# Chained waits between GpSimd's compute operations, in a fused linear-attention, Fourier-mix and MLP kernel

## Chip, cores and metric

The kernel runs on one core of a Trainium2 chip. The metric is device time in microseconds (us) for one execution, lower is better. Engines are named as in the profile: PE is TensorE, DVE is VectorE, ACT is ScalarE, POOL is GpSimd, SP is the engine that issues most transfers.

## What is computed

A gated linear attention over 768 steps feeds a Fourier mix, a layer norm and an MLP, for 4 batches:

```python
for t in range(S):                                   # S = 768, 8 heads of 48
    cur = einsum('bhd,bhe->bhde', u * k[t], v[t])
    y[t] = einsum('bhd,bhde->bhe', r[t], state + cur)
    state = w * state + einsum('bhd,bhe->bhde', k[t], v[t])
x = y as [4, 768, 384]
un = layer_norm(x + real(fft(fft(x, axis=1), axis=2)))
out = (x + mixed) + relu(un @ w_ch1) @ w_ch2         # 384 -> 1536 -> 384
```

## The kernel before

The sequence is cut into chunks of 128 steps, 24 in all (6 for each of 4 batches). For one chunk, `attend` multiplies k and r by tables of powers of w (tile KR, line 385), transposes them (on PE, line 409, or by a transposing transfer of SP, line 415; tile KRT), forms the scores (line 443), masks them (AC and MA, lines 450 to 455), and adds the masked product with V (line 534), the carried state S (line 513) and the bonus of u (PR at line 431, de at line 507 with the small table UW, TT at line 522) into one bank. The result is X. The chunks of a batch are folded by even and odd symmetry (EO, HH, XF, lines 557 to 593), go through the two Fourier products (lines 635 and 676, with tiles TT2 and TR), and become UF, its scaled copy UB (line 700 on POOL) and, transposed (line 720 on PE with the copy at line 727, or by SP at line 746), UNT. The MLP then runs by halves of a batch: `mlp1` at line 764, `mlp2` at line 785, the result osb at line 795 and its transfer out at line 798.

No scheduler decides the order. Each operation is recorded with one or more alternatives (an engine, a key, a function), and the long table `ORDER` lists number and alternative in the order of issue; `_Schedule.emit` walks it, assigns buffers of the rings to tiles and calls the function. Each engine then runs its instructions in that order, and waits on semaphores are set where one instruction reads, or writes over, what another made. Instructions of one engine are not made to wait for the one just ahead unless such a dependence is found.

POOL has 91 compute operations (copies, masks, products) and issues 24 transfers: four small ones of w and u into the tile wuc at the start (line 301), five of the MLP's weights (lines 839 and 842), and 15 of results. wuc is used on DVE, where UW is formed (line 338), and on ACT, where the logarithm lwc is taken (line 329). An instruction carries one wait; where it needs more, the others stand in a wait instruction (EVENT_SEMAPHORE) ahead of it.

Of the kernel before, what the change touches and what calls it, by code (L numbers as in the profile page):

```python
# [9 lines left out]
AluOp = mybir.AluOpType  # L10
# [5 lines left out]
H = 8  # L16
S = 768
D = 48
# [33 lines left out]
class _Tile:  # L52


    def __init__(self, ring, view=None):
        self.ring, self.view, self.value = ring, view, None
# [5 lines left out]
class _Schedule:  # L62


    def __init__(self):
        self.ops, self.rings = [], {}

    def ring(self, name, tiles):
        self.rings[name] = tiles
# [1 line left out]
    def op(self, name, alts, r=(), w=(), new=(), use=(), after=(), uses=None, link=None):  # L71
        self.ops.append(dict(name=name, alts=alts, r=list(r), w=list(w), new=list(new), use=list(use), after=list(after),
                             uses=uses or [[] for _ in alts], link=link))

    def emit(self, order):
        last = {}
        for k, (n, a) in enumerate(order):
            o = self.ops[n]
            for t in o["new"] + o["use"] + o["uses"][a]:
                last[t] = k  # L80
        held = {name: [-1] * len(tiles) for name, tiles in self.rings.items()}
        for k, (n, a) in enumerate(order):
            o = self.ops[n]
            for t in o["new"]:
                ends = held[t.ring]
                m = min(range(len(ends)), key=ends.__getitem__)
                assert ends[m] < k, (o["name"], t.ring)
                ends[m] = last[t]
                t.value = self.rings[t.ring][m] if t.view is None else t.view(self.rings[t.ring][m])
            fn = o["alts"][a][2]  # L90
            if fn is not None:
                fn()


ORDER = """
# [74 lines left out]
def kernel(  # L170
# [11 lines left out]
    nc = tc.nc  # L182
# [5 lines left out]
    hid_c = nc.inline_tensor(hid_n, name="hid_c")  # L188

    sch = _Schedule()  # L190
    op = sch.op
    sch.ring("bank", [ps.tile([128, 512], F32, name=f"bank{i}") for i in range(8)])

# [60 lines left out]
    def T(name, view=None):  # L254
        return _Tile(name, view)
# [115 lines left out]
    def attend(i):  # L371
# [3 lines left out]
        KR, V, KRT, PR = T("KR"), T("V"), T("KRT"), T("PR")  # L375
# [3 lines left out]
        def scaled(s):  # L379
            return (KR()[:, s].rearrange("t p (a d) -> t (p a) d", a=2)[:, :, 0:D], kr()[:, s],  # L380
                    wtab[ph][:, s].rearrange("t (h d) -> t h d", d=D))

        def scale(eng, s):
            o, x, y = scaled(s)
            eng.tensor_tensor(out=o, in0=x, in1=y, op=AluOp.mult)  # L385

        def both():
            nc.vector.tensor_tensor(
# [6 lines left out]
        for s, nm in ((0, "k"), (1, "r")):  # L395
            dve = ("DVE", "K1", lambda s=s: scale(nc.vector, s))
            pool = ("POOL", "K1", lambda s=s: scale(nc.gpsimd, s))
            op(("KR", i, s), [VOID, dve, pool if s else dve, dve if s else pool], r=[(nm, i), ("wt", ph, s)] + zeroed,
               w=[("KR", i, s)], use=[kr, KR], after=[("KR", i)], link=("KR", i))
# [11 lines left out]
        for s, dn in ((0, kdone), (1, qdone)):  # L411
# [4 lines left out]
            out=KRT().rearrange("d s p t -> d (s p) t"), in_=KR().rearrange("t s p c -> t (s p c)")))],  # L416
# [86 lines left out]
        DE, TT = T("DE"), T("TT")  # L503
# [15 lines left out]
           uses=[[yd], []])  # L519

        def spread(eng, x):
            eng.tensor_tensor(out=TT(), in0=V(), in1=x.unsqueeze(2).to_broadcast([128, H, D]), op=AluOp.mult)

        op(("TT", i), [("POOL", "TT", lambda: spread(nc.gpsimd, DE())), ("DVE", "TTp", lambda: spread(nc.vector, yd()[:, DM:]))],
           r=[("DE", i), ("V", i), ("de", i)], w=[("TT", i)], new=[TT], use=[V], uses=[[DE], [yd]], link=("DE", i))
        if q > 0:
            one(("qs", i), "PE", "qs", carried, r=[("S", i), ("de", i)] + kts, use=[yd, St, KRT])

        def intra():
# [13 lines left out]
            out=X()[:, q, :], in0=yd()[:, 0:DM], in1=TT().rearrange("p h d -> p (h d)"), op=AluOp.add)),  # L543
# [76 lines left out]
    def fourier(b):  # L620
        X, XF = bat[b]["X"], bat[b]["XF"]
        TT, TR = T("TT2"), T("TR")
# [28 lines left out]

        def rev(g):
            def turn(eng):
                eng.tensor_copy(TR()[0:97, 2 * g:2 * g + 2, :], TT()[0:97, 2 * g:2 * g + 2, 384:0:-1])

            op(("TR", b, g), [("DVE", "TR", lambda: turn(nc.vector)), ("POOL", "TR", lambda: turn(nc.gpsimd)),
                              ("ACT", "TR", lambda: nc.scalar.copy(
                                  TR()[0:97, 2 * g:2 * g + 2, :], TT()[0:97, 2 * g:2 * g + 2, 384:0:-1]))], w=[("TR", b, g)],
                r=[("TT2", b, 2 * g), ("TT2", b, 2 * g + 1)], new=[TR] if g == 0 else [], use=[TR, TT],
                after=[("TR", b, 0)] if g else [])  # L660
# [70 lines left out]
        for sh in range(2):  # L731
# [12 lines left out]
            for j in range(3):  # L744
                turned(sh, j, UB, UNT)
            op(("UNT", b, sh), [VOID, VOID, VOID, VOID, ("SP", "xbar9", lambda UB=UB, UNT=UNT: nc.sync.dma_start_transpose(
                out=UNT().rearrange("p j c t -> p (j c) t"), in_=UB().rearrange("p j d -> p (j d)")))],
# [79 lines left out]
    for i in range(NC):  # L827
# [5 lines left out]
                  out=tn_t, in0=te_t[:, :, :, 1, :], scalar1=-1.0, scalar2=None, op0=AluOp.mult))], r=["te"], w=["tn"])  # L833
# [4 lines left out]
    for n in range(2):  # L838
        one(("W1", n), "POOL", "dma_w1", lambda n=n: nc.gpsimd.dma_start(
            out=W1[:, :, n * 768:(n + 1) * 768], in_=w1[:, n * 768:(n + 1) * 768].rearrange("(c p) f -> p c f", p=128)))  # L840
    for n in range(3):
        one(("W2", n), "POOL", "dma_w2", lambda n=n: nc.gpsimd.dma_start(
            out=W2[:, n * 4:(n + 1) * 4, :], in_=w2[n * 512:(n + 1) * 512, :].rearrange("(p f) d -> p f d", f=4)))
# [37 lines left out]
```

## Time and profile before

| | us |
|---|---|
| median of 3 runs | 174.22 (174.11 to 176.03) |
| the profiled execution | 174.01 |
| its span, first to last instruction | 172.3 |
| PE busy | 155.3 |
| DVE busy | 136.6 |
| ACT busy | 108.2 |
| POOL busy | 82.0 |

The profiled execution is 174.01 us; 1.7 us of it lies outside the span. Times in rows are us from the span's start. A row of a timeline gives start, duration, engine, line, operation, and, in brackets, how long the engine sat idle ahead of it and what ended that. The matmuls' ends are modelled, so that a busy PE is one that has been fed, not one at its peak.

### The profile page before, as it was taken

How to read it: one execution, taken by the hardware profiler on the slowest of the kernel's cores; microseconds unless marked ns; L12 is line 12 of the kernel's file. 1: busy time of each engine (PE TensorE's matmuls, PEld its weight loads, DVE VectorE, ACT ScalarE, POOL GpSimd, SP SyncE). 2: the span in 40 equal slices, each digit the busy share in tenths (PEclk: the TensorE clock that was granted, in tenths of full speed). 3: DMA queues.
4: the chain of work that ended last, by engine and by line, in shares of the span. 5: the costliest groups of instructions: out<-in, count | busy, mean ns of one | idle time of the engine just before them, and what ended most of it. 6: DMA issues, size and time to landing. Idle time of an engine off the chain costs nothing.

```text
span 172.3 us, 4247 instructions
## 1 busy us (share of the span) xinstructions
PE 155.3 (90%) x1586; PEld 111.6 (65%) x1586; DVE 136.6 (79%) x320; ACT 108.2 (63%) x258; POOL 82.0 (48%) x119
## 2 busy tenths in 40 slices
PE   4367977689999999999999999999999999999990
PEld 1155755559767776877666687677776876666670
DVE  4489999987798989999579999968899689630460
ACT  2976786448988697656993577578861850922400
POOL 7277387814828980778376473466330122000131
PEclk9999999978999999999999999999999999999999
DMA  5999999999698999999999959999500236200132
GB/s 115 212 209 212 232 200 242 149 189 201 119 198 173 188 166 173 221 212 212 216 187 237 214 104 194 237 199 181 200 3 0 94 68 181 73 4 0 46 137 91
DMA packets 97782, 27.08 MB, mean 157 GB/s; under 512 B 94369, under 2 KB 96434, under 8 KB 97762
## 3 DMA queue, kind: packets, MB, share of 16 engines
q1 hardware_dynamic: 92336, 21.01, 63.0%
q0 software_dynamic: 2304, 5.21, 13.0%
q10 hardware_dynamic: 3122, 0.59, 2.1%
q8 instruction: 12, 0.20, 0.5%
q14 instruction: 8, 0.07, 0.1%
HBM read 19.77 MB, written 4.72 MB: 142 GB/s over the span
## 4 chain that ended last, share of the span: by engine, by line
PE 54%; issue 23%; DVE 11%; DMA 4%; POOL 4%; SPq 1%; POOLq 0%; ACT 0%; DVEq 0%
PE bank L764 19%; PE bank L785 14%; DMA kr<-in_r_dram 4%; PE bank L635 4%; PE bank L676 3%; PE bank L443 3%; PE bank L409 2%; DVE KR L385 2%; POOL out_dram L798 2%; PE bank L474 2%; PE bank L534 2%; PE bank L513 2%; DVE MA L455 1%; DVE XF L566 1%; DVE PR L431 1%
## 5 line engine op out<-in xcount | busy, mean ns | idle before, releaser
L764 PE MATMUL bank<-UNT,W 128*128 128x384 bf16 x288 | 54.8, 327 | 0.0
L785 PE MATMUL bank<-W,HT 128*128 128x384 bf16 x276 | 52.0, 326 | 0.0
L769 ACT ACTIVATE HT<-bank 128x384 bf16<-128x384 f32 x73 | 33.5, 491 | 21.8 <-PE bank L764 21.6
L764 PEld LDWEIGHTS <-W 128*128 128x128 bf16 x288 | 30.5, 114 | 11.7
L785 PEld LDWEIGHTS <-HT 128*128 128x128 bf16 x276 | 25.8, 98 | 14.1
L385 DVE TENSOR_TENSOR KR<-kr,wtab 128x384 bf16<-128x384 f32 x30 | 21.4, 727 | 3.8 <-ACT wtab L325 2.9
L798 POOL DMA_DIRECT2D out_dram<-osb x14 | 8.0, 572 | 33.9 <-DVE osb L795 33.9
L452 POOL TENSOR_SCALAR_AFFINE_SELECT MA<-AC 128x512 bf16<-128x512 bf16 x25 | 16.3, 657 | 8.7 <-ACT AC L450 8.6
L385 POOL TENSOR_TENSOR KR<-kr,wtab 128x384 bf16<-128x384 f32 x14 | 15.2, 1090 | 10.6 <-DMA kr<-in_r_dram 5.0
L795 DVE SCALAR_TENSOR_TENSOR osb<-bank,rstd,UF 128x384 f32<-128x384 f32 x23 | 13.5, 610 | 7.9 <-PE bank L785 6.8
L450 ACT CAST AC<-bank 128x512 bf16<-128x512 f32 x25 | 14.2, 587 | 6.8 <-PE bank L443 5.8
L770 DVE TENSOR_SCALAR HT<-bank 128x384 bf16<-128x384 f32 x23 | 12.3, 548 | 6.8 <-PE bank L764 6.7
L455 DVE TENSOR_TENSOR MA<-bank,mtri 128x512 bf16<-128x512 f32 x23 | 15.3, 680 | 1.1 <-PE bank L443 1.1
L409 PE MATMUL bank<-ident,KR 128*128 128x128 bf16 x112 | 12.0, 253 | 3.9 <-DVE UW L311 1.8
L419 ACT COPY KRT<-bank 128x512 bf16<-128x512 bf16 x20 | 11.2, 589 | 5.2 <-PE bank L409 5.0
L635 PE MATMUL bank<-te_t,XF 128*128 128x193 bf16 x108 | 12.2, 251 | 2.1 <-DVE XF L566 1.2
L409 PEld LDWEIGHTS <-KR 128*128 128x128 bf16 x112 | 8.8, 114 | 6.4 <-DVE UW L311 3.0
L431 POOL TENSOR_TENSOR PR<-KRT 128x512 bf16<-128x512 bf16 x7 | 8.1, 1156 | 10.2 <-ACT KRT L419 9.7
L707 ACT ACTIVATE tn_t<-UF,sm 128x384 bf16<-128x384 f32 x21 | 12.9, 613 | 0.1
L635 PEld LDWEIGHTS <-XF 128*128 128x128 bf16 x120 | 10.4, 100 | 3.5 <-DVE XF L566 1.6
L688 DVE SCALAR_TENSOR_TENSOR UF<-bank,X 128x384 f32<-128x384 f32 x21 | 11.0, 552 | 1.6 <-PE bank L676 1.6
L542 DVE TENSOR_TENSOR X<-bank,TT 128x384 bf16<-128x384 f32 x18 | 9.6, 550 | 2.6 <-PE bank L534 2.5
(110 smaller groups left out, 259.8 us busy)
## 6 DMA issues: line engine op xcount, KB each, us to landing
kr<-in_k_dram SPq DMA_DIRECT2D x23, 192.0 KB, 4.1
kr<-in_r_dram SPq DMA_DIRECT2D x23, 192.0 KB, 4.1
vt<-in_v_dram SPq DMA_DIRECT2D x23, 192.0 KB, 4.2
out_dram<-osb POOLq DMA_DIRECT2D x14, 192.0 KB, 3.0
out_dram<-osb SPq DMA_DIRECT2D x9, 192.0 KB, 2.5
W<-in_moe_w_ch_dram POOLq DMA_DIRECT2D x2, 576.0 KB, 8.4
W<-in_moe_w_ch_dram POOLq DMA_DIRECT2D x3, 384.0 KB, 5.6
te_t<-te_c SPq DMA_DIRECT2D x1, 579.0 KB, 5.9
```

The source lines that it names most:

```text
L385: eng.tensor_tensor(out=o, in0=x, in1=y, op=AluOp.mult)
L409: nc.tensor.transpose(tps[s]()[:, p, :], KR()[:, s, p, :], ident)
L450: op(("AC", i, a), [("ACT", "AC", lambda: nc.scalar.copy(AC(), A_ps[a]())), ("NONE", "", None)], r=[("A", i)], w=[("AC", i, a)], new=[AC], ...
L452: op(("MA", i, a), [("POOL", "MA", lambda: nc.gpsimd.affine_select(out=MA[a](), in_=AC(), pattern=[[0, NP], [1, 128]], base=0, channel_mul ...
L455: ("DVE", "MA", lambda: nc.vector.tensor_tensor(out=MA[a](), in0=A_ps[a](), in1=mtri.unsqueeze(1).to_broadcast([128, NP, 128]), op=AluOp.m ...
L635: nc.tensor.matmul(fp()[:, par, :], lhsT=lhsT[:, g * CH:g * CH + 128], rhs=rhs, start=(nb == 0 and par == 0), stop=(nb == last and par == ...
L707: ("ACT", "SQ", lambda: nc.scalar.activation(out=squares, in_=UF()[:, j, :], func=Act.Square, scale=-float(DM), bias=sm()[:, j:j + 1], acc ...
L764: nc.tensor.matmul(hp(), lhsT=W1[:, dt, ft // 4 * 512 + ft % 4:(ft // 4 + 1) * 512:4], rhs=UNT()[:, :, dt, :], start=(dt == 0), stop=(dt = ...
L769: op(("HT", hf, ft), [("ACT", "HT", lambda: nc.scalar.activation(out=HT()[:, ft, :], in_=hp(), func=Act.Relu, scale=-1.0)), ("DVE", "HT", ...
L770: ("DVE", "HT", lambda: nc.vector.tensor_scalar(out=HT()[:, ft, :], in0=hp(), scalar1=-1.0, scalar2=0.0, op0=AluOp.mult, op1=AluOp.max))],
L785: nc.tensor.matmul(mo(), lhsT=HT()[:, ft, j * 128:(j + 1) * 128], rhs=W2[:, ft, :], start=(ft == 0), stop=(ft == 11))
L795: one(("osb", hf, j), "DVE", "osb", lambda: nc.vector.scalar_tensor_tensor(out=osb(), in0=mo(), scalar=rstd()[:, j:j + 1], in1=UF()[:, j, ...
```

## The change

Each compute operation of POOL is given a wait for POOL's compute operation ahead of it, and where POOL has issued one or more transfers in between, an empty instruction (`engine_nop`) is put behind them, and the next compute operation waits for that one. The order of everything else stays.

```diff
-            fn = o["alts"][a][2]
+            eng, key, fn = o["alts"][a]
             if fn is not None:
-                fn()
+                if eng != "POOL":
+                    fn()
+                elif key.startswith("dma"):
+                    fn()
+                    self.issued = True
+                else:
+                    self.chain(fn, self.issued)
+                    self.issued = False
...
+    last = []
+
+    def chain(fn, issued):
+        if issued:
+            last.append(nc.gpsimd.engine_nop())
+        made = fn()
+        if last:
+            tc.add_manual_dep(made.ins, last[-1].ins.name,
+                              mybir.DependencyInfo(mybir.DependencyClass.Sync, mybir.DependencyReason.DATA),
+                              reason="all cores of GpSimd done")
+        last.append(made)
+
+    sch.chain = chain
...
-            eng.tensor_tensor(out=o, in0=x, in1=y, op=AluOp.mult)
+            return eng.tensor_tensor(out=o, in0=x, in1=y, op=AluOp.mult)
```

Three helpers (`scale`, `spread`, `turn`) return their instruction, so that it can be chained. In the built program, 89 of the 91 compute operations wait for POOL's own semaphore (Pool_49) where 16 did, 15 empty instructions are new, and POOL's wait instructions go from 48 to 97. The programs of PE, DVE, ACT and SP have the same instructions in the same order, with waits on the same semaphores.

At the start of POOL's program, where the four transfers into wuc stand among the first fills (S_98 and the like are buffers; DVE_49, Activation_49, DMAHW4_49 the semaphores of DVE, ACT and a transfer), before:

```order
L301 DMA wuc<-in_u_dram 48x4x1 [waits DVE_49]
L319 MEMSET S_98 128x384
L301 DMA wuc<-in_w_dram 48x4x1
L288 AFFINE_SELECT ident<-HT_186 128x128 [waits DVE_49]
L319 MEMSET S_95 128x384
L301 DMA wuc<-in_u_dram 48x4x1
```

and now, lines counted in the changed kernel (ISA at L202 is the empty instruction):

```order
L321 DMA wuc<-in_u_dram 48x4x1 [waits DVE_49]
L202 ISA
L339 MEMSET S_98 128x384 [waits Pool_49]
L321 DMA wuc<-in_w_dram 48x4x1
L202 ISA
L308 AFFINE_SELECT ident<-HT_186 128x128 [waits DVE_49,Pool_49]
L339 MEMSET S_95 128x384 [waits Pool_49]
L321 DMA wuc<-in_u_dram 48x4x1
```

Two empty instructions and three waits now stand ahead of the third transfer into wuc.

On POOL again, at the first blocks of UB (batch 0, ahead of the first MLP product), before:

```order
L431 TENSOR_TENSOR PR_123<-KRT_120 128x512 [waits Activation_49]
L700 TENSOR_SCALAR UB_179<-UF_148,sm_163 128x384 [waits Activation_49]
L700 TENSOR_SCALAR UB_179<-UF_148,sm_163 128x384 [waits DVE_49]
L700 TENSOR_SCALAR UB_180<-UF_149,sm_164 128x384 [waits Activation_49]
L522 TENSOR_TENSOR TT_141<-V_117,DE_138 128x384 [waits Activation_49]
```

and now:

```order
L451 TENSOR_TENSOR PR_123<-KRT_120 128x512 [waits Activation_49,Pool_49]
L720 TENSOR_SCALAR UB_179<-UF_148,sm_163 128x384 [waits Activation_49,Pool_49]
L720 TENSOR_SCALAR UB_179<-UF_148,sm_163 128x384 [waits DVE_49,Pool_49]
L720 TENSOR_SCALAR UB_180<-UF_149,sm_164 128x384 [waits Activation_49,Pool_49]
L542 TENSOR_TENSOR TT_141<-V_117,DE_138 128x384 [waits Activation_49,Pool_49]
```

The order is the same; each has a second wait, for its predecessor on POOL, and so a wait instruction ahead of it for the first one.

## Rows read from the trace of the kernel before

**Rows 1.** The page's busy times: engine, busy us, share, instructions.
```profile
PE 155.3 (90%) x1586; PEld 111.6 (65%) x1586; DVE 136.6 (79%) x320; ACT 108.2 (63%) x258; POOL 82.0 (48%) x119
```

**Rows 2.** Busy time by stretch: window, its length, busy us of each engine.
```profile
9.40:36.00 26.60, 19.62 (x276) 15.22 (x273) 25.88 (x59) 17.93 (x41) 18.64 (x28) 1.00 1.08 206
36.00:46.00 10.00, 9.96 (x133) 8.42 (x131) 8.44 (x23) 8.06 (x22) 4.54 (x7) 0.83 0.98 179
46.00:126.00 80.00, 80.00 (x863) 57.28 (x862) 70.92 (x153) 60.41 (x147) 47.82 (x63) 1.00 0.97 191
```

**Rows 3.** Timeline of POOL, the start, with the transfers into wuc.
```profile
1.54 0.77 POOL L301 DMA_DIRECT2D wuc<-in_u_dram  x1 [0.50 <-DVE wuc L295]
2.31 0.44 POOL L319 MEMSET S<- 128x384 bf16 x1
2.67 0.60 POOL L301 DMA_DIRECT2D wuc<-in_w_dram  x1
3.28 0.30 POOL L288 TENSOR_SCALAR_AFFINE_SELECT ident<-HT 128x128 bf16<-128x128 bf16 x1
3.53 0.42 POOL L319 MEMSET S<- 128x384 bf16 x1
3.89 0.61 POOL L301 DMA_DIRECT2D wuc<-in_u_dram  x1
```

**Rows 4.** The tile wuc: its transfers from issue to landing.
```profile
DMA to landing us min/median/max: 4.3/5.2/5.4
```

**Rows 5.** Timeline of DVE where it uses wuc.
```profile
9.42 0.16 DVE L338 TENSOR_TENSOR UW<-wuc 64x4 bf16<-64x4 f32 x1 [0.29 <-DMA wuc<-in_u_dram]
9.75 0.56 DVE L385 TENSOR_TENSOR KR<-kr,wtab 128x384 bf16<-128x384 f32 x1 [0.17 <-DMA kr<-in_r_dram]
```

**Rows 6.** Timeline of POOL, two XF in a row, the second waiting for the first.
```profile
28.35 0.51 POOL L566 TENSOR_TENSOR XF<-HH 128x196 bf16<-128x196 bf16 x1 [0.93 <-DVE HH L560]
...
28.94 0.57 POOL L566 TENSOR_TENSOR XF<-HH 128x196 bf16<-128x196 bf16 x1
```

**Rows 7.** The chain of waits near 24 and 125 us: start, us, what.
```profile
23.55 0.07 issue
23.61 0.51 POOL XF L566
...
124.88 0.02 POOLq L522
124.90 0.10 issue
```

**Rows 8.** Timeline of POOL, very small fills at the program's start.
```profile
0.31 0.10 POOL L865 MEMSET const-float32-0.0<- 128x1 f32 x1 [0.31 <-issue]
0.34 0.10 POOL L865 MEMSET const-float32-1.0<- 128x1 f32 x1
```

**Rows 9.** Timeline of POOL at the first blocks of UB.
```profile
40.85 1.16 POOL L431 TENSOR_TENSOR PR<-KRT 128x512 bf16<-128x512 bf16 x1 [5.74 <-ACT KRT L419]
41.99 0.58 POOL L700 TENSOR_SCALAR UB<-UF,sm 128x384 bf16<-128x384 f32 x1
...
42.70 0.59 POOL L700 TENSOR_SCALAR UB<-UF,sm 128x384 bf16<-128x384 f32 x1
```

**Rows 10.** Timeline of PE, the transposes of those blocks.
```profile
42.72 0.33 PE L720 MATMUL bank<-ident,UB 128*128 128x128 bf16 x3
...
43.34 0.51 PE L720 MATMUL bank<-ident,UB 128*128 128x128 bf16 x6
```

**Rows 11.** Timeline of POOL, then of PE, at a mask in the dense stretch.
```profile
52.74 0.64 POOL L452 TENSOR_SCALAR_AFFINE_SELECT MA<-AC 128x512 bf16<-128x512 bf16 x1
...
53.88 0.36 PE L534 MATMUL bank<-V,MA 128*128 128x48 bf16 x8
```

**Rows 12.** Timeline of DVE near 116 us.
```profile
116.37 0.55 DVE L522 TENSOR_TENSOR TT<-V,bank 128x384 bf16<-128x384 bf16 x1 [0.53 <-POOL V L402]
```

More of the change, by code (lines that the diff above doesn't have):

```diff
@@ L65, in __init__ @@
     def __init__(self):
-        self.ops, self.rings = [], {}
+        self.ops, self.rings, self.issued = [], {}, False
     def ring(self, name, tiles):
@@ L521, in spread @@
         def spread(eng, x):
-            eng.tensor_tensor(out=TT(), in0=V(), in1=x.unsqueeze(2).to_broadcast([128, H, D]), op=AluOp.mult)
+            return eng.tensor_tensor(out=TT(), in0=V(), in1=x.unsqueeze(2).to_broadcast([128, H, D]), op=AluOp.mult)
         op(("TT", i), [("POOL", "TT", lambda: spread(nc.gpsimd, DE())), ("DVE", "TTp", lambda: spread(nc.vector, yd()[:, DM:]))],
@@ L653, in turn @@
             def turn(eng):
-                eng.tensor_copy(TR()[0:97, 2 * g:2 * g + 2, :], TT()[0:97, 2 * g:2 * g + 2, 384:0:-1])
+                return eng.tensor_copy(TR()[0:97, 2 * g:2 * g + 2, :], TT()[0:97, 2 * g:2 * g + 2, 384:0:-1])
             op(("TR", b, g), [("DVE", "TR", lambda: turn(nc.vector)), ("POOL", "TR", lambda: turn(nc.gpsimd)),
```

## The prediction

> **What bounds the kernel now.** I read the busy times first: PE is busy 155.3 of 172.3 us, POOL 82.0 [rows 1]. The share is an average, so I read the busy times by stretch next. From 46 to 126 us PE is busy 80.00 of 80.00 us, and from 36 to 46 us 9.96 of 10.00: there PE's own stream, in a fixed order, sets the end, and whatever delays it once is not won back. From 9.4 to 36 us DVE is busy 25.88 of 26.60 us, PE only 19.62: there DVE's stream sets when the first Fourier products and so the MLP can begin [rows 2]. POOL is never the busiest engine. So a slower POOL costs time only where DVE or PE stands waiting for something that POOL made or sent, and the question is where that is with less cover than POOL is late.
>
> **What one wait costs.** Two operations in a row without a wait: the second starts before the first one's row ends, by 0.05 us (3.28 + 0.30 against 3.53) [rows 3] or 0.02 (40.85 + 1.16 against 41.99) [rows 9]. The trace holds one pair in which the second already waits for the first: 28.35 + 0.51 = 28.86, and it starts at 28.94, 0.08 us later [rows 6]. So a wait between neighbours that are both ready costs 0.08 + 0.05 = 0.13 us (0.10 with the smaller overlap).
>
> Where POOL stood idle for another engine, the wait for its predecessor is long met, but the other engine's semaphore is now awaited in a wait instruction of its own. Directly, an operation starts 0.07 us after its release; through a wait instruction 0.02 + 0.10 = 0.12 us after that instruction began [rows 7]. That costs 0.05 us.
>
> An empty instruction is not in the trace of before. The nearest rows are fills of one element: 0.10 us long, but started 0.03 us apart [rows 8]. I take 0.10, because a wait sees the end and not the start, and 0.08 for the wait behind it: 0.18 us, since the fill behind a transfer starts now just as the transfer's row ends (1.54 + 0.77 = 2.31) [rows 3]. From below it could be nothing, if the empty instruction overlaps; from above I bound it by the transfer's own row, 0.77 + 0.08 = 0.85 us. The row of the small fill is nearer in kind, as neither moves data, so 0.18 stands.
>
> In total POOL gets at most 89 x 0.13 + 15 x 0.10 = 13 us more, 95 of 172 us: it does not become the bound by its sum. What counts are two places.
>
> **Place one, the transfers into wuc.** Ahead of the third transfer stand now two empty instructions and one wait between neighbours (select, then fill); the transfers themselves wait for nothing new. It is issued 2 x 0.18 + 0.13 = 0.49 us later than at 3.89 [rows 3]. Such transfers take 4.3 to 5.4 us to land [rows 4], and DVE waits for one of them: it sat idle 0.29 us ahead of UW at 9.42. So nothing covers the 0.49 us there; but the operation after next, KR at 9.75, sat idle 0.17 us for its own transfer, which now swallows 0.17 [rows 5]. What is left on DVE is 0.49 - 0.17 = 0.32 us. Queued behind UW on DVE is everything that PE needs. In the stretch to 36 us DVE is idle 0.72 us, of which the two gaps named are 0.46; the other 0.26 [rows 2, 5] could swallow most of it if those gaps are waits for transfers or for an engine that has not moved; I take it that PE, fed by DVE, moves along, and keep 0.32, with 0.06 as the low end. ACT, too, takes a logarithm of wuc; its delay runs beside that of DVE and is not added.
>
> **Place two, the first UB.** PR at 40.85 was released by ACT: now through a wait instruction, +0.05. UB at 41.99 follows it directly: +0.13. It ends at 42.75 instead of 42.57, and PE's transposes of it, at 42.72 now [rows 9, 10], begin 0.18 us later. The second UB then starts at 42.75 + 0.08 = 42.83 instead of 42.70, +0.13 [rows 9]; its transposes at 43.34 [rows 10] have by then moved 0.18 with PE's stream, so this is covered. +0.18 us, in a stretch where PE has no idle time to give [rows 2].
>
> **Elsewhere.** After 46 us I found no product of POOL for which PE waits. The closest is a mask that ends at 52.74 + 0.64 = 53.38 and is used at 53.88: 0.50 us of cover [rows 11], against one wait of 0.13. The masks, copies and products around it come in runs of two to four between idle times of POOL, so lateness of 0.3 to 0.5 us builds up and is given back. DVE waits once, 0.53 us at 116.37 [rows 12], where the copy that it needs comes 0.05 us later; DVE has 9 us idle in that stretch [rows 2]. I cost all this at nothing; if its cover fails at one place, that is 0.1 to 0.4 us. The last transfers have no compute operation of POOL behind them, hence no empty instruction.
>
> **Sum.** 0.32 + 0.18 = 0.50 us. On the profiled execution, 174.01 us (span 172.3 and 1.7 around it), that makes 174.5; the median of the runs is 0.2 us above that execution, so I forecast 174.7 us, which a measurement of this kernel can hardly tell from no change (2% is about 3.5 us).
>
> [...] With a free empty instruction the first place gives 0.13, less than the 0.17 of cover, and the sum is 0.18 us.
>
> **Rivals.**
> - *All hidden, or the waits cost nothing.* The empty instruction is free, 0.13 us at wuc stays under the 0.17 of cover, and UB's 0.18 is all: 174.22 + 0 to 0.18, 174.3 us. For it: the gaps of DVE that I left out, 0.26 us. Against it: the pair of XF shows a price [rows 6]. That the change does not do what it says, because neighbours were in order anyway, would end here too.
> - *A dear empty instruction.* It takes as long as the transfer ahead of it, 0.85 us with its wait: 2 x 0.85 + 0.13 - 0.17 = 1.66, and 0.18: 176.1 us. For it: the transfer's row is made on the same engine. Against it: the fill behind a transfer starts at the row's end and takes 0.44 us, hardly more than the 0.42 of the other one [rows 3], so the engine is free by then.
> - *The empty instruction is held until its transfer has landed*, and this makes the kernel slower. Landing takes 5.2 us [rows 4], the row ahead 0.77 and 0.60, so each of the two adds some 4.5 us, and UW comes 2 x 4.5 + 0.13 later: 9.1 - 0.17 + 0.18 = 9.1 us, 183.3 us. It decides the sign from 1.7 us per empty instruction, where 2 x 1.7 + 0.13 - 0.17 + 0.18 reaches 3.5. Against it: only the fill's start at the row's end, which shows that the engine, not that an empty instruction, is free.
> - *Faster*: kept apart, operations of POOL disturb one another or DVE less. If each of the 89 were 0.01 us shorter on a path, 0.5 us at best after the waits: 173.7 us. Against it: the XF that waits is longer, 0.57 against 0.51 [rows 6].
>
> **Chances.** The forecast (174.4 to 175.4) 0.50; hidden 0.24; dear 0.13; landed 0.05; faster 0.05, hardly ever by 2%; and 0.03 for covers that fail in several places of the dense stretch at once, some 178 us. The range takes the low end from the faster rival and the high end just beyond the dear one: 173.8 to 176.4 us. Slower by over 2%: 0.05 for landing and 0.02 of the failing covers, 0.07; faster by over 2%: 0.01; within it 0.92.
>
> **What would show it.** Right: neighbours on POOL 0.08 us apart instead of overlapping; rows behind transfers some 0.18 us later; the third transfer into wuc near 4.4 us, UW near 9.9, DVE's XF ahead of the Fourier products 0.3 us later, PE's first transposes of UB 0.5 us later than 42.72, and no idle time of PE between 46 and 126 us. Wrong: UW still near 9.4, so that place one is empty; gaps behind transfers of 0.5 us or more; idle time of PE in the dense stretch ended by POOL.

## The result: slightly faster, where 0.5 us slower was forecast

The changed kernel takes 172.08 us (median of 17 runs; 170.56 to 175.90) beside 175.67 us for the kernel before on the same chip (17 runs; 172.12 to 177.29, and one of 311.81). The ratio, with disturbed runs of either kernel left out, is 0.9893, with a 95% interval of 0.9846 to 0.9939: about 1.1% or 1.9 us faster. The forecast was 0.5 us slower.

The profiled execution of the changed kernel took 174.44 us, 2.4 us more than its median; what it lost on the way is told under *No idle time of PE*. Its busy times on the page and its busy times by stretch, columns as in [rows 1, 2]:

```profile
PE 154.9 (90%) x1586; PEld 110.4 (64%) x1586; DVE 134.7 (78%) x320; ACT 108.2 (63%) x258; POOL 84.0 (49%) x119
```

```profile
9.40:36.00 26.60, 20.96 (x293) 16.37 (x292) 25.87 (x61) 19.07 (x44) 18.64 (x27) 1.00 1.00 196
36.00:46.00 10.00, 9.15 (x123) 7.39 (x123) 8.21 (x24) 8.49 (x26) 5.97 (x9) 1.00 1.07 197
46.00:126.00 80.00, 78.49 (x846) 55.70 (x844) 68.82 (x152) 58.48 (x142) 47.85 (x60) 1.00 0.98 192
```

POOL is 2.0 us busier and DVE 1.9 us less busy, though both ran the same operations. In the second pair of traces (before_again and after_again, below) POOL is 2.6 us busier again, but DVE is 0.3 us busier too, so its saving in the first pair does not repeat over the whole span. From 9.4 to 36 us PE works through 293 matmuls instead of 276 [rows 2], and 295 instead of 274 in the second pair. And the granted clock (the last column but two) is 1.00 from 36 to 46 us, where it was 0.83.

What the prediction described on POOL is there. Timeline of POOL at the start, answering [rows 3]:

```profile
1.54 0.77 POOL L321 DMA_DIRECT2D wuc<-in_u_dram  x1 [0.50 <-DVE wuc L315]
2.40 0.42 POOL L339 MEMSET S<- 128x384 bf16 x1
2.77 0.60 POOL L321 DMA_DIRECT2D wuc<-in_w_dram  x1
3.47 0.29 POOL L308 TENSOR_SCALAR_AFFINE_SELECT ident<-HT 128x128 bf16<-128x128 bf16 x1
3.82 0.42 POOL L339 MEMSET S<- 128x384 bf16 x1
4.18 0.60 POOL L321 DMA_DIRECT2D wuc<-in_u_dram  x1
```

The fill behind a transfer starts 0.09 us after its row ends (2.40 against 1.54 + 0.77), where it started with no gap; neighbours stand 0.06 us apart (3.47 + 0.29 = 3.76, then 3.82) where they overlapped. The third transfer is issued 0.29 us later. Timeline of DVE, answering [rows 5]:

```profile
9.67 0.16 DVE L358 TENSOR_TENSOR UW<-wuc 64x4 bf16<-64x4 f32 x1 [0.68 <-DMA wuc<-in_u_dram]
9.89 0.66 DVE L405 TENSOR_TENSOR KR<-kr,wtab 128x384 bf16<-128x384 f32 x1
```

UW comes 0.25 us later. So the delay at wuc is real, and yet the kernel is faster: something else gave back more. It stands near 32 us. The kernel before was run once more beside the changed one (before_again); its timelines of POOL, DVE and PE there:

```profile
31.37 0.81 POOL L839 DMA_DIRECT2D W<-in_moe_w_ch_dram  x1
32.18 0.52 POOL L402 CAST V<-vt 128x384 bf16<-128x384 f32 x1
32.63 0.81 POOL L839 DMA_DIRECT2D W<-in_moe_w_ch_dram  x1
33.46 1.08 POOL L385 TENSOR_TENSOR KR<-kr,wtab 128x384 bf16<-128x384 f32 x1
```

```profile
31.93 1.76 DVE L431 TENSOR_TENSOR PR<-KRT 128x512 bf16<-128x512 bf16 x1
33.88 1.69 DVE L566 TENSOR_TENSOR XF<-HH 128x196 bf16<-128x196 bf16 x3
35.49 1.02 DVE L385 TENSOR_TENSOR KR<-kr,wtab 128x384 bf16<-128x384 f32 x2
```

```profile
33.74 0.25 PE L507 MATMUL bank<-UW,PR 128*128 128x2 bf16 x4 [1.23 <-DVE PR L431]
35.63 0.26 PE L635 MATMUL bank<-te_t,XF 128*128 128x193 bf16 x1 [0.86 <-DVE XF L566]
```

and those of the changed kernel:

```profile
31.82 0.81 POOL L859 DMA_DIRECT2D W<-in_moe_w_ch_dram  x1
32.73 0.50 POOL L422 CAST V<-vt 128x384 bf16<-128x384 f32 x1
33.18 0.80 POOL L859 DMA_DIRECT2D W<-in_moe_w_ch_dram  x1
34.09 1.05 POOL L405 TENSOR_TENSOR KR<-kr,wtab 128x384 bf16<-128x384 f32 x1
```

```profile
32.38 0.41 DVE L451 TENSOR_TENSOR PR<-KRT 128x512 bf16<-128x512 bf16 x1
32.98 0.83 DVE L586 TENSOR_TENSOR XF<-HH 128x196 bf16<-128x196 bf16 x3
33.73 1.83 DVE L405 TENSOR_TENSOR KR<-kr,wtab 128x384 bf16<-128x384 f32 x2
```

DVE's product PR took 1.76 us beside POOL's two W1 transfers and the copy and product behind them, and the three XF 1.69 us; now they take 0.41 and 0.83. An operation that takes longer like this, without a wait that the profile shows, is called held below. PE waited for exactly these two, 1.23 and 0.86 us; it no longer waits for them. One hold is left: the two KR behind XF take 1.83 us where they took 1.02. So DVE is spared 1.35 + 0.86 - 0.81 = 1.40 us near 32 us.

A second part is the clock. In the first profile of the kernel before, PE's stretch right behind those two waits reads (columns as in [rows 2]):

```profile
36.20:39.60 3.40, 3.40 (x31) 2.73 (x29) 2.57 (x7) 1.71 (x3) 0.00 (x0) 0.50 1.15 196
```

Half the full clock, 0.50 where it was 1.00 from 9.4 to 36.2 us, for 3.4 us, after PE had stood idle for DVE twice, 1.22 and 0.86 us in this profile. before_again has the same two waits, and in the same stretch the full clock, 1.00:

```profile
36.20:39.60 3.40, 3.40 (x56) 3.00 (x54) 3.35 (x9) 2.89 (x6) 0.18 (x1) 1.00 1.16 200
```

So the half clock followed the two waits in one of the two executions only.

### The profile page after: what moved, and what is told of

The parts are those of the page before. It is cut to its first block, busy times and chain, and to the rows that moved or that the text cites. A ratio compares the mean times of both kernels' runs of the same rounds, so it can differ in the third digit from the quotient of the medians.

```text
span 172.7 us, 4311 instructions
## 1 busy us (share of the span) xinstructions
PE 154.9 (90%) x1586; PEld 110.4 (64%) x1586; DVE 134.7 (78%) x320; ACT 108.2 (63%) x258; POOL 84.0 (49%) x119
## 4 chain that ended last, share of the span: by engine, by line
PE 51%; issue 17%; DVE 11%; DMA 10%; POOL 7%; SPq 1%; ACT 1%; POOLq 1%; DVEq 0%; ACTq 0%
PE bank L784 17%; PE bank L805 14%; DMA kr<-in_r_dram 6%; PE bank L655 5%; PE bank L696 4%; DMA wuc<-in_u_dram 3%; PE bank L463 3%; POOL out_dram L818 2%; PE bank L554 2%; PE bank L494 2%; POOL XF L586 2%; DVE KR L405 2%; PE bank L429 2%; DVE XF L622 1%; PE bank L533 1%
## 5 line engine op out<-in xcount | busy, mean ns | idle before, releaser
L405 DVE TENSOR_TENSOR KR<-kr,wtab 128x384 bf16<-128x384 f32 x30 | 19.7, 673 | 5.1 <-ACT wtab L345 2.9
L451 POOL TENSOR_TENSOR PR<-KRT 128x512 bf16<-128x512 bf16 x7 | 9.7, 1383 | 6.1 <-ACT KRT L439 5.2
L655 PEld LDWEIGHTS <-XF 128*128 128x128 bf16 x120 | 9.9, 97 | 2.0 <-DVE XF L586 0.7
```

Source lines behind the costliest of these rows:

```text
L405: return eng.tensor_tensor(out=o, in0=x, in1=y, op=AluOp.mult)
L655: nc.tensor.matmul(fp()[:, par, :], lhsT=lhsT[:, g * CH:g * CH + 128], rhs=rhs, start=(nb == 0 and par == 0), stop=(nb == last and par == ...
```

## The experiments

Theory A, the collision theory of after_again's expectation: POOL's operation behind a transfer that POOL issues holds up DVE's products already while the transfer's row runs, so that such a product is held for long, as PR was for 1.76 us. The empty instruction with its wait puts that off, so that the hold is short. It is the author's conjecture; what happens inside POOL is in no row. Rivals: the gaps between neighbours, which the pair waits open, let DVE in (B); luck of phase, since everything moved by a few tenths (C).

**before_again** and **after_again**: both kernels once more.

> The kernel before, once more, for a second trace of it. [...] Luck theory (the long PR was an accident of one execution): PR takes 0.4 to 0.6 us and the time moves by 1 to 2 us.

> The changed kernel, once more, for a second trace. Collision theory: ratio 0.985 to 0.992; DVE's PR behind the first weight transfer takes 0.41 us again, PE's first MLP product starts 1.5 to 2.5 us earlier than in the trace of before, and no half clock near 36 us. Luck theory: the ratio scatters around 1.00.

Measured: the kernel before 175.06 us (median of 10; ratio to the shared runs of the kernel before 0.997, 0.991 to 1.003); changed 172.63 us (median of 10; 0.995, 0.991 to 0.999). PR took 1.76 us again in the one and 0.41 us again in the other, so this is no accident of one profile. The gain is measurable again, but smaller, and smaller than expected (0.985 to 0.992). The two profiled executions took the same time, 172.53 us each, although in the changed one PE's first transposes of UB start 1.07 us earlier (40.14 against 41.21 us). What becomes of that lead is told further down.

**nops_only** and **waits_only**: one half of the change each.

```diff
# nops_only: only the operation behind a transfer waits
-        if last:
+        if issued:
             tc.add_manual_dep(made.ins, last[-1].ins.name,
# waits_only: every operation waits for the one ahead, no empty instruction
-        if issued:
-            last.append(nc.gpsimd.engine_nop())
```

> Empty instructions behind POOL's transfers and the wait of the next operation for them, but no waits between neighbouring compute operations. [...] Theory B (the gaps of 0.08 us between neighbours let DVE in): no gain, ratio 0.998 to 1.005, PR 1.2 us or more. Theory C (any shift of a few tenths changes which operations collide): in between, other collisions than in either trace.

> Waits between POOL's compute operations, but no empty instructions: an operation behind a transfer waits only for the compute operation ahead of the transfer. Theory A: no gain, or the few tenths that the waits cost: ratio 0.998 to 1.005, PR on DVE behind the first weight transfer 1.2 us or more. Theory B: the whole gain, ratio 0.985 to 0.992. Theory C: in between.

Measured: nops_only 172.56 us, ratio 0.992 (0.987 to 0.996), PR 0.41 us, where theory A was given 171.5 to 172.5 us, 0.985 to 0.992 and 0.41 us. waits_only 174.06 us, ratio 1.000 (0.996 to 1.004). Timelines of DVE and PE in waits_only:

```profile
32.12 1.06 DVE L449 TENSOR_TENSOR PR<-KRT 128x512 bf16<-128x512 bf16 x1
33.37 2.20 DVE L584 TENSOR_TENSOR XF<-HH 128x196 bf16<-128x196 bf16 x3
```

```profile
33.23 0.25 PE L525 MATMUL bank<-UW,PR 128*128 128x2 bf16 x4 [0.59 <-DVE PR L449]
35.63 0.28 PE L653 MATMUL bank<-te_t,XF 128*128 128x193 bf16 x1 [1.37 <-DVE XF L584]
```

The holds have moved from PR to XF, but their sum is nearly the same: 1.06 + 2.20 = 3.26 us against 3.45. PE waits 1.96 us against 2.09. PR in waits_only is shorter than the 1.2 us that was expected, because part of the hold falls on XF. The gain is in the empty instructions and the waits for them; B falls.

**w1_only, all_but_w1, w1_fill**: which empty instructions, and is it the instruction or the delay?

```diff
# w1_only: nops_only, with
+                    self.issued = key == "dma_w1"
# all_but_w1: the full change, with
+                    self.issued = key != "dma_w1"
# w1_fill: as w1_only, but no wait, and in place of the empty instruction
+            nc.gpsimd.memset(next(gap), 0.0)      # one element
```

> [...] The PR product of DVE near 32 us takes 0.4 to 0.5 us instead of 1.77, PE is 2.0 to 2.6 us earlier than in the profile of before by 40 us, ratio 0.985 to 0.994. Rival (the gain is spread over many small collisions on DVE, or comes from the waits between neighbours): PR may be short, but PE is less than 1 us earlier and the ratio is 0.997 to 1.003.

> The same kernel as w1_only, whose runs were too much disturbed to compare. Theory A (the two W1 transfers carry the gain): PR near 32 us 0.4 to 0.5 us, PE 2.0 to 3.2 us earlier at 40 us than in the profile of before, ratio 0.985 to 0.995. Rival (what is won there is given back whole, since later loads set the pace): PE earlier at 40 us as well, but within 0.5 us of before from 70 us on, ratio 0.997 to 1.003.

> The change in full, without the empty instructions behind the two W1 transfers (the operations behind them wait for the compute operation ahead of the transfer). Theory A: PR of DVE near 32 us takes 1.0 us or more again, PE is 0 to 0.5 us later than before at 40 us, ratio 0.998 to 1.005. Rival (waits and gaps all over do it): PR short, PE 2 us earlier, ratio 0.990 to 0.996.

> [...] Theory A: PR near 32 us still takes 1.0 us or more, ratio 0.997 to 1.004. Rival (luck of phase: any delay of 0.1 to 0.2 us there makes DVE and POOL miss one another): PR takes 0.4 to 0.6 us, PE 2 us earlier, ratio 0.986 to 0.994.

Measured: w1_only gave 176.62 us (median of 6, 172.46 to 188.03) and no ratio; PR took 0.41 us there. w1_only_2, the same kernel, gave 173.54 us (median of 6, 171.31 to 177.77), ratio 0.982 (0.976 to 0.989). This ratio rests on three of its six runs, and the two medians of all runs are closer, 173.54 against 174.98 us; taken with w1_only, it is weak evidence. all_but_w1: 173.63 us, 0.999 (0.994 to 1.004). w1_fill: 174.62 us, 1.002 (0.996 to 1.008). DVE near 32 us in w1_only_2, all_but_w1 and w1_fill:

```profile
31.69 0.41 DVE L451 TENSOR_TENSOR PR<-KRT 128x512 bf16<-128x512 bf16 x1
32.29 0.85 DVE L586 TENSOR_TENSOR XF<-HH 128x196 bf16<-128x196 bf16 x3
```

```profile
31.61 1.06 DVE L451 TENSOR_TENSOR PR<-KRT 128x512 bf16<-128x512 bf16 x1
32.85 2.20 DVE L586 TENSOR_TENSOR XF<-HH 128x196 bf16<-128x196 bf16 x3
```

```profile
31.62 0.72 DVE L446 TENSOR_TENSOR PR<-KRT 128x512 bf16<-128x512 bf16 x1
32.52 2.73 DVE L581 TENSOR_TENSOR XF<-HH 128x196 bf16<-128x196 bf16 x3
```

The small fill without a wait does not do it (0.72 + 2.73 = 3.45 us, as before; PR alone is below the 1.0 us expected), and neither do the other thirteen empty instructions (1.06 + 2.20 us). This speaks against C, and so does the phase: in all eleven traces PR starts 0.55 to 0.57 us after the first W1 transfer, with the long PR and with the short one. But the fill put off the copy behind that transfer by 0.04 us only, the empty instruction by 0.10; a delay of 0.10 us without a wait was not tried. How much PE gains up to 40 us is read best from the start of DVE's PR to PE's first transposes of UB, since this leaves out what differs ahead of it:

| kernel | PR starts, us | transposes of UB, us | between |
|---|---|---|---|
| before_again | 31.93 | 41.21 | 9.28 |
| all_but_w1 | 31.61 | 40.87 | 9.26 |
| w1_fill | 31.62 | 40.89 | 9.27 |
| w1_only_2 | 31.69 | 39.49 | 7.80 |
| nops_only | 32.43 | 40.22 | 7.79 |
| nops_not_wuc (below) | 31.89 | 39.69 | 7.80 |
| changed | 32.38 | 40.21 | 7.83 |
| changed, second run | 32.31 | 40.14 | 7.83 |
| before, with the half clock | 31.88 | 42.72 | 10.84 |
| waits_only, with slow clock there | 32.12 | 42.95 | 10.83 |

Up to here the two empty instructions behind W1 are worth 1.43 to 1.49 us in every kernel that has them, close to the 1.40 us that DVE is spared, and the slow stretch of the clock costs 1.55 to 1.58 us where it occurs (w1_only is left out, as its clock was at 0.85 throughout). all_but_w1 misses its expectation on PE (0.34 us earlier than before_again, not later), because PR starts 0.32 us earlier there. The rows behind two of these lines, PE's first transposes of UB in w1_only_2 and in all_but_w1:

```profile
39.49 0.33 PE L740 MATMUL bank<-ident,UB 128*128 128x128 bf16 x3
```

```profile
40.87 0.34 PE L740 MATMUL bank<-ident,UB 128*128 128x128 bf16 x3
```

At the end of the program less of this is left. The span of the profiled execution is 170.8 us in before_again and in all_but_w1, which lack the two empty instructions; with them it is 170.8 us in the second run of the changed kernel, 170.1 in nops_only, 170.0 in w1_only_2 and 170.4 in nops_not_wuc. So nothing to 0.8 us of the lead reaches the end in these traces, while the half clock in the first profile of before (172.3 us) does cost 1.5 us there. That the kernels with the two empty instructions are faster as a whole is shown by the ratios of nops_only and nops_not_wuc beside those of waits_only, all_but_w1 and w1_fill.

**pair_alone** and **pair_parts**: the collision by itself, without the kernel around it. DVE computes products like PR back to back; POOL runs short patterns beside it.

```diff
# pair_parts: a section is 7 products of DVE and, beside them, one of these on POOL
+        for ops in ("K", "D", "DK", "DNK", "DM", "DFK", "DnK", "DK", "DNK"):
# K product like KR, D transfer like W1, N empty instruction that the next waits for,
# n empty instruction alone, M large fill, F fill of one element
```

> Leaves the reference's computation out altogether: DVE does products like PR (two SBUF tiles, 128x512 bf16) back to back, beside POOL in four patterns, each at two phases: one copy; two copies and two products like KR; copy, transfer, copy, transfer, product; the same with the empty instruction and its wait behind each transfer. Theory A: DVE's product takes 0.40 to 0.45 us alone; in the third pattern one of them is held for over 1.2 us across transfer and copy; in the fourth none takes over 1.0 us, and the DVE products of a section end earlier by 0.5 us or more. [...] Rival (only phase): which of the two is longer changes between the two phases.

> Leaves the reference's computation out: seven DVE products like PR in a row, and beside them on POOL, in this order of sections: product K alone; transfer alone; transfer and K; transfer, empty instruction, K that waits for it; transfer and a large fill (reads nothing); transfer, fill of one element, K; transfer, empty instruction, K without the wait; then the third and the fourth once more. [...] The one-element fill behaves like transfer and K. Rival (the transfer itself holds DVE): the section with the transfer alone shows a product of 0.7 us or more. Rival (K is simply longer behind a transfer): one long product of 1.6 to 2.0 us.

pair_alone: beside copy, transfer, copy, transfer, product, DVE's ten products took 5.6 and 5.3 us without the empty instructions and 4.8 and 3.4 us with them. In the first pair two products took 1.21 us without them and one did with them. The forecast of none over 1.0 us in the chained pattern was wrong: the product of POOL holds DVE once in any case. The second pair is blurred, because there DVE held POOL's first copy for 3.7 us.

pair_parts is clean. Timeline of DVE and POOL for the sections K (from 3.07 us), D (6.42), D K (9.06), D N K (13.09), D M (16.52) and D n K (23.20):

```profile
3.07 3.16 DVE L70 TENSOR_TENSOR PR<-x 128x512 bf16<-128x512 bf16 x7
...
6.42 2.44 DVE L70 TENSOR_TENSOR PR<-x 128x512 bf16<-128x512 bf16 x7 [0.19 <-POOL gap L95]
7.16 0.93 POOL L78 DMA_DIRECT2D W<-in_moe_w_ch_dram  x1 [0.77 <-DVE PR L70]
...
9.06 3.84 DVE L70 TENSOR_TENSOR PR<-x 128x512 bf16<-128x512 bf16 x7 [0.19 <-POOL gap L95]
9.79 0.78 POOL L78 DMA_DIRECT2D W<-in_moe_w_ch_dram  x1 [0.77 <-DVE PR L70]
10.59 1.00 POOL L89 TENSOR_TENSOR V<-kf,wf 128x384 bf16<-128x384 f32 x1
...
13.09 3.24 DVE L70 TENSOR_TENSOR PR<-x 128x512 bf16<-128x512 bf16 x7 [0.19 <-POOL gap L95]
13.81 0.80 POOL L78 DMA_DIRECT2D W<-in_moe_w_ch_dram  x1 [0.76 <-DVE PR L70]
14.73 0.99 POOL L89 TENSOR_TENSOR V<-kf,wf 128x384 bf16<-128x384 f32 x1
...
16.52 2.44 DVE L70 TENSOR_TENSOR PR<-x 128x512 bf16<-128x512 bf16 x7 [0.19 <-POOL gap L95]
...
23.20 3.87 DVE L70 TENSOR_TENSOR PR<-x 128x512 bf16<-128x512 bf16 x7 [0.19 <-POOL gap L95]
```

Seven products take 2.44 us beside a transfer alone, and as much beside a transfer and a large fill, which reads nothing: in these two sections the transfer did not hold DVE. A reading product of POOL adds about 0.7 to 0.8 us (3.16 and 3.24). The same product behind a transfer adds 1.40 us (3.84), while POOL's own row is not longer for it (1.00 against 0.99). With the wait it is 0.80 again; with the empty instruction but no wait 1.43 (3.87), and with the one-element fill 1.42 (3.86). D K and D N K, run once more at the end, gave 3.85 and 3.25. Theory A was given two products of 1.2 us in D K, so two holds of 0.8 us; one came that runs through, and D K is 0.6 us longer on DVE than D N K (3.84 against 3.24). The held product of DVE in the section D K:

```profile
10.07 1.82 DVE L70 TENSOR_TENSOR PR<-x 128x512 bf16<-128x512 bf16 x1
```

It ends at 11.89 us. At its usual 0.42 us it would have ended at 10.49, 0.1 us before POOL's product has its row (10.59): so the hold begins, 0.1 to 0.5 us ahead of that row, while only the transfer's row is shown. One long product of 1.6 to 2.0 us is what was expected of the rival that POOL's product is simply longer behind a transfer. What speaks against it is POOL's row, which is as long as with the wait.

That DVE is held while the transfer's row runs is shown (from 10.49 us at the latest, POOL's product having its row at 10.59), and that with the wait 0.80 of the 1.40 us are left. That POOL's next operation is what holds it by then is inferred: the same transfer holds nothing when a fill follows it (2.44 us). How that operation could act ahead of its row no run shows.

**nops_not_wuc**: a version that might beat both.

```diff
# nops_only, with
+                    self.issued = key != "dma_wuc"
```

> The empty instruction and its wait behind every transfer but the four into wuc at the start, no waits between neighbours: 13 fewer causes of delay at the start than the change. If the prediction's first place is right, UW comes near 9.4 us again and not 9.7, so PE is 0.25 to 0.36 us earlier than in the changed kernel by 20 us; ratio 0.985 to 0.993, the fastest of the versions. Rival (loads set the pace behind 60 us): the 0.3 us are lost there, ratio as that of nops_only, 0.988 to 0.996.

Measured: 172.40 us (median of 6; 171.12 to 173.40), ratio 0.985 (0.979 to 0.991), against 174.98 us for the kernel before in the same series. It beats the kernel before; over the changed kernel (0.989, 0.985 to 0.994; 0.995, 0.991 to 0.999) it is not shown to be faster, as its interval overlaps with the first of these and meets the second. UW came at 10.09 us, not 9.4, behind a DVE product that took 1.78 us from 7.84 on: that step of the expectation failed. PE's first transposes of UB come at 39.69 us, 0.52 earlier than in the changed kernel.

## Why the prediction was wrong

*What bounds the kernel* held near 32 us: PE is fed by DVE's stream, and what DVE is spared there PE has at 40 us. Earlier it did not hold: in nops_not_wuc UW comes 0.67 us later than in the kernel before, and PE's products behind the first XF start at 30.52 us, as before (30.51). And the step after it, "a slower POOL costs time only where DVE or PE stands waiting for something that POOL made or sent", is the one that failed. It left out a third way in which POOL acts on DVE: by working at the same time (a product of POOL beside seven of DVE cost these 0.7 to 0.8 us in pair_parts). DVE's 25.88 us of busy time [rows 2] were taken for work. 1.36 us of them were one product standing still (and 0.86 us more the three XF), and the trace of before showed it; the group of that line and operation on DVE, by form:

```profile
L431 DVE TENSOR_TENSOR PR<-KRT 128x512 bf16<-128x512 bf16 x13 | 7.1, 549 | 0.0
```

Thirteen products, 549 ns on average: with one of 1.77 us among them, the other twelve come to (7.1 - 1.77) / 12 = 0.45.

*The empty instruction* was priced at 0.18 us and cost 0.09. That it isn't free was right; what was not seen is that with the wait for it POOL's next operation holds DVE for a shorter time, 0.80 instead of 1.40 us in pair_parts.

*The pair wait*, priced at 0.13 us, was right: 0.05 + 0.06 = 0.11 at the start. At UB, in the second run of the changed kernel, POOL reads

```profile
38.23 1.16 POOL L451 TENSOR_TENSOR PR<-KRT 128x512 bf16<-128x512 bf16 x1 [2.24 <-ACT KRT L439]
39.50 2.64 POOL L720 TENSOR_SCALAR UB<-UF,sm 128x384 bf16<-128x384 f32 x4
```

38.23 + 1.16 = 39.39, and UB starts at 39.50: 0.11 us of gap where there were 0.02 of overlap [rows 9], 0.13 in all.

*Place one*: the third transfer 0.29 us later (0.49 forecast), UW 0.25 later, and PE's products behind the first XF start at 30.83 us instead of 30.51: 0.32 us, the net figure of the sum. That it agrees is luck. The terms are smaller, in the second pair it is 0.21 us (30.76 against 30.55), and all_but_w1, which has the same start as the changed kernel and UW at 9.74 us, has these products at 30.06, earlier than either kernel before (on another chip). What the delay of UW costs PE is not shown.

*Place two*: the two terms of POOL are there, but PE came to UB 2.5 us earlier (40.21 against 42.72 [rows 10]), so that what was left of the 0.18 us can't be read.

*Elsewhere, costed at nothing*: this is the term that was put at nothing and decided the sign. At 40 us it is minus 1.43 to 1.49 us, by the table above, and some 1.55 us more against executions in which the clock fell there. The rival "faster" named the mechanism, operations of POOL that "disturb one another or DVE less", and sized it at 0.01 us on each of 89 operations. (That is 0.89 us; less the 0.50 us of the forecast it leaves 0.39 us and 173.8 us, the low end of the range, and not the 173.7 us given there.) It is nearly 1.5 us at two of them, and not from keeping operations apart but from the empty instruction behind a transfer.

*No idle time of PE between 46 and 126 us* was wrong in the profile of the changed kernel, where part of the lead is lost again. DVE, then PE:

```profile
65.62 0.56 DVE L405 TENSOR_TENSOR KR<-kr,wtab 128x384 bf16<-128x384 f32 x1 [1.51 <-DMA kr<-in_r_dram]
```

```profile
66.24 0.40 PE L429 MATMUL bank<-ident,KR 128*128 128x128 bf16 x4 [1.25 <-DVE KR L405]
```

In that execution, 174.44 us, the lead was spent and more. In the second one (172.53 us) one wait of PE, ended by DVE, took 0.62 us:

```profile
59.31 0.65 PE L784 MATMUL bank<-UNT,W 128*128 128x384 bf16 x3 [0.62 <-DVE MA L475]
```

Two other kernels with a lead wait once at the same products: PE waits 0.7 us for a transfer in w1_only_2, 1.0 us for ACT in nops_not_wuc. So the lead at 40 us, 1.0 to 1.07 us net (0.38 to 0.45 us are given to the later start of PR), does not add up to a fixed gain at the end; against before_again nothing of it was left. That the two measured gains, 1.1% and 0.5%, differ would fit a kernel before that runs with or without the slow stretch of the clock: in the series with both kernels, 13 of 35 executions of before and none of 10 of the changed one had a mean granted clock of 0.987 or less (3 of 17 of the changed one in the first series). Against it stands that 6 of the 12 executions of w1_only and w1_only_2 had such a clock, too, though they have the two empty instructions. Whether the waits of PE bring the clock down, and how often, was not tried by itself. So the sign is explained, but how much of the 1.9 us is the hold and how much the clock stays open.

## What to carry to other kernels

Before costing waits, compare each group's longest instruction with its shortest: a DVE operation that takes four times its usual time beside POOL's (1.77 against 0.41 us here) is a wait that no view lists as one. Where POOL issues transfers between its copies and products, as the two of W1 here, try an empty instruction and a wait on it behind the transfer: each cost 0.09 us of POOL here, and the two spared DVE 1.40. Put it where DVE's products are on the path that feeds PE; ahead of transfers for which somebody waits it costs, as at UW, which came 0.25 us later. And follow a lead to the end of the program: the one of 1.07 us at 40 us was gone there.

## What the runs showed of the hardware beyond that

- A wait for the compute operation ahead of a transfer is not enough (PR and the three XF took 3.26 us in waits_only and in all_but_w1, 3.45 before and 1.24 with the change), and an empty instruction for which nobody waits isn't either (3.87 against 3.24 us).
- The hold works both ways: in pair_alone, a copy of POOL that takes 0.50 us took 3.75 us while DVE ran ten products back to back.
- In pair_parts neither a transfer of POOL by itself nor a transfer and a large fill held DVE (2.44 us both times); the sections with a product of POOL, which reads two tiles, took 3.16 to 3.87 us.
